# Strassen products chained in one PSUM bank with ScalarE copies, and another division of the preparing work

## The chip, the cores and the metric

The kernel runs on one core of a Trainium2 chip. Such a core has a matrix engine (TensorE, in the profile PE, its weight loads PEld), VectorE (DVE), ScalarE (ACT), GpSimd (POOL) and SyncE (SP), which work side by side, each through its own queue in order, and wait for one another through semaphores. Operands lie in SBUF (128 partitions); TensorE writes its products into the eight banks of PSUM. The metric is the device time of one execution in microseconds, lower is better.

## The reference

An attention layer feeds a layer of experts:

```
scores = q k^T / 8 in a window of +-15, joined with 24 block scores (q against the maximum of k over 32 rows)
a      = softmax(scores);  attn = a [v; mean of v over blocks]        # batch 4, 8 heads, 768 rows, 64 wide
x      = attn as (3072, 512)
noisy  = x w_gate + log1p(exp(x w_noise)) * noise                     # (3072, 8)
top2, weights = the two largest of noisy per row, softmax over the two
for e in range(8):
    for the rows whose top2 holds e:
        h = relu(x[rows] @ w1[e])                                     # 512 -> 1024
        out[rows] += weight * (h @ w2[e])                             # 1024 -> 512
```

All inputs and outputs are float32.

## The kernel before

**Attention and routing** fill the first part. They write x to DRAM (`xd`) as a pair of 16-bit floats, high part and remainder, and make a table that lists, for every expert, the rows that it takes, with their weights. Each expert has 816 slots (`CAP`), in seven chunks of 128 rows, the last of 48.

**The expert part** runs over e = 0 to 7. Every 32-bit operand is a pair of 16-bit floats, a high one and a low one (`...h`, `...l`), and every product is made of three passes: high by high, low by high, high by low. For one expert:

- `x_gather` (GpSimd's queue, an indirect DMA into one of four buffers `xg`) and `x_trans` (SP's queue, a transposing DMA) bring x into `xte`, transposed, for two experts alternately.
- `w_load` (SP's queue) brings the weights in eight pieces through four staging buffers `stg`: w1 in four, then w2 in four.
- The first matmul, h = relu(x w1), uses one level of Strassen's scheme (Winograd's form) for experts 1 to 7: seven products of half-size blocks in place of eight. It needs sums of blocks of w1 (`ws`, split into `sh` and `sl`), and sums of blocks of x (`tt`, split into `tx`).
- The second matmul, y = h w2, goes chunk by chunk: three passes of eight matmuls (`mm2_turn`, line 890; line 887 for the last chunk). `y_out` (VectorE, line 913) multiplies by the row's weight and adds `prev`, what `out` held for those rows, which `prev_gather` has fetched by an indirect DMA of GpSimd's queue; `y_scatter` writes the rows back in the same way. The bank `pt` has two buffers, so a chunk waits for `y` of the chunk before last.

**The first matmul in detail.** `mm1_quad(e, f, tick)` makes group f (0 to 3), which is rows f and f+4 of h. A `product` is six matmuls of 128 x 408 columns. It calls products 1, 6, 5, 7, 4, 2, 3. Products 1 and 2 go to bank `a`, 6 and 7 to `b`, 5 and 3 to `d`, 4 to `c`, where the second of a pair adds onto the first:

```
p1 = copy(a)  after 1 (ScalarE);   u2 = b + p1  after 6;   u3 = b + p1  after 7  (VectorE)
c2 = [c + u3 | d + u3]  after 4;   c1 = d + u2  after 3
```

Product 7 adds into `b`, so TensorE has to wait until `u2` has been read from it. `h_split` then makes the high part of h (ScalarE, `relu`, line 815) and the low one (VectorE, line 818).

**The order of the work** is written by hand. After each product and after each pass of the second matmul a `tick` is counted: ticks 0 to 27 lie in the first matmul (28 = `M2`), 28 to 48 in the second. `put(e, k, f, ...)` hangs a call on tick k of expert e, and the instruction goes into its engine's queue there. So the next expert n = e+1 is prepared while e runs:

- `w1_sums` (lines 653 to 656): four sums on GpSimd for each of two pairs of pieces of w1, ticks 18 and 34.
- `w1_pair` (lines 669 and 671): high parts on ScalarE, low parts on VectorE, of plain blocks (part 0) and of sums (part 1).
- `t_diff` (line 688): GpSimd subtracts blocks of x, of the high and of the low part; `t_join`, `t_two` (line 676) and `t_four` (699 and 676) add on VectorE; `t_hi` (709, ScalarE) and `t_lo` (676, VectorE) split into `tx`.
- `STEPS` has fourteen groups of these calls. For n from 2 on the first two (`t_diff` of 3, high and low) sit at ticks 20 and 21, the other twelve at ticks 28 to 39, one on each.
- w1 is loaded in the first matmul, w2 at ticks 34, 35, 39 and 40, and split by `w_split` (lines 629 and 646) at ticks 3, 10, 17 and 24 of its own expert.
- x of n is gathered at ticks 1, 3, ... 13 of e's first matmul.

Expert 0 has plain matmuls without Strassen's scheme. Its ticks 3 to 10 follow the second half of its first matmul, 11 to 22 the passes of its chunks 3 to 6; expert 1 is prepared there.

Of the kernel before, what the change touches and what calls it, by code (L numbers as in the profile page):

```python
# [20 lines left out]
P = 128  # L21
# [39 lines left out]
def attn_moe(ctx, tc, qt, kt, vt, wgn, noise, w1, w2, out):  # L61
# [586 lines left out]
    WS_ = {}  # L648
# [9 lines left out]
    def w1_pair(e, k, part):  # L658
        w = WT[e]
        hi, lo = w["w1h"], w["w1l"]  # L660
        if part == 0:
            todo_ = [(hi[:, k, :HF], lo[:, k, :HF], SG[e, k][:, :HF]),
                     (hi[:, k + 2], lo[:, k + 2], SG[e, k + 2])]
        else:
            s = WS_[e, k]
            todo_ = [(w["sh"][:, :, k], w["sl"][:, :, k], s[:, 0:3]),
                     (hi[:, k, HF:], lo[:, k, HF:], s[:, 3])]
        for h, _, x in todo_:
            nc.scalar.activation(h, x, AF.Copy, scale=W1S)  # L669
        for h, l, x in todo_:  # L670
            nc.vector.scalar_tensor_tensor(l, x, W1S, h, op0=OP.mult, op1=OP.subtract)  # L671
# [3 lines left out]
    def plus(o, a, b, op=OP.add):  # L675
        nc.vector.scalar_tensor_tensor(o, a, 1.0, b, op0=OP.mult, op1=op)  # L676

    def tt(e, j):
        TT[e, j] = side_pool[0].tile([P, 2, HC], F32, name="tt", bufs=3)
        return TT[e, j]  # L680
# [4 lines left out]
    def t_diff(e, j, low):  # L685
        i = (1, 1) if j == 3 else (0, 1)
        o = (0, 1) if j == 3 else (0, 0)
        nc.gpsimd.tensor_tensor(tt(e, (j, low)), xb(e, *i, low), xb(e, *o, low), op=OP.subtract)  # L688
# [16 lines left out]
    def t_of(e, j):  # L705
        return TT[e, (j, 0)] if j in (1, 3) else TT[e, 2]
# [106 lines left out]
    def h_split(f, c0, c1, c, hook=None):  # L813
        hh, hl = HT
        nc.scalar.activation(hh[:, f, c0:c1], c, AF.Relu)  # L815
        if hook:
            hook()
        nc.vector.scalar_tensor_tensor(hl[:, f, c0:c1], c, 0.0, hh[:, f, c0:c1], op0=OP.max, op1=OP.subtract)  # L818

    def mm1_quad(e, f, tick):  # L820
        def temp(name, n=HC):
            return side_pool[0].tile([P, n], F32, name=name)

        a = accs[0].tile([P, 512], F32, name="a")[:, :HC]
        product(a, e, f, 1, True, False)
        p1 = temp("p1")
        nc.scalar.activation(p1, a, AF.Copy)  # L827
        tick()
        b = bank()[:, 0, :HC]
        product(b, e, f, 6, True, False)  # L830
        u2 = temp("u2")
        nc.vector.tensor_add(u2, b, p1)  # L832
        tick()
        d = bank()[:, 0, :HC]
        product(d, e, f, 5, True, False)
        tick()
        product(b, e, f, 7, False, True)
        u3 = temp("u3")
        nc.vector.tensor_add(u3, b, p1)  # L839
        c2 = temp("c2", 2 * HC)  # L840
        nc.vector.tensor_add(c2[:, HC:], d, u3)
        tick()
        c = bank()[:, 0, :HC]
        product(c, e, f, 4, True, True)
        nc.vector.tensor_add(c2[:, :HC], c, u3)  # L845
        h_split(f + FC // 2, 0, CAP, c2)
        tick()
        product(a, e, f, 2, False, True)
        h_split(f, 0, HC, a)
        tick()  # L850
        product(d, e, f, 3, False, True)
# [53 lines left out]
    def y_out(e, c, pv):  # L905
        py = PY[c]
        d = HD if c == LAST else DM
        y = side_pool[0].tile([P, DM], F32, name="y", bufs=4)[:, :d]
        gw = (TL[:, e] if c == LAST else tb_of(e, c)).bitcast(F32)[:, 1:2]
        if pv is None:  # L910
            nc.vector.tensor_scalar(y, py[:, :d], gw, None, op0=OP.mult)
        else:
            nc.vector.scalar_tensor_tensor(y, py[:, :d], gw, pv[:, :d], op0=OP.mult, op1=OP.add)  # L913
        y_scatter(e, c, y)
# [293 lines left out]
    STEPS = (
        ((t_diff, 3, 0),),
        ((t_diff, 3, 1),),  # L1210
        ((t_alloc,), (t_join, 3), (t_hi, 3)),
        ((t_two, 0),),
        ((t_two, 1), (t_lo, 3), (t_hi, 2)),
        ((w1_pair, 0, 0), (t_diff, 1, 0)),
        ((t_lo, 2), (t_diff, 1, 1)),
        ((w1_pair, 0, 1),),
        ((t_four,), (t_hi, 4)),
        ((t_lo, 4),),
        ((w1_pair, 1, 0),),
        ((t_join, 1), (t_hi, 1)),  # L1220
        ((w1_pair, 1, 1),),
        ((t_lo, 1),),
    )

    def steps(e, where, ks):
        for k, fs in zip(ks, STEPS):
            for f, *a in fs:
                put(where, k, f, e, *a)
# [5 lines left out]
    put(0, 8, w1_sums, 1, 0)  # L1234
    steps(1, 0, (9, 9, 10, 10, 11, 12, 12, 13, 14, 15, 16, 17, 19, 20))
    put(0, 13, w1_sums, 1, 1)
    for i, k in enumerate((14, 15, 20, 21)):
        put(0, k, w_load, 1, 4 + i)
    M2 = 7 * (FC // 2)
    for e in range(1, E):  # L1240
        put(e, 0, w2_alloc, e)
        for i in range(4):
            put(e, 7 * i + 3, w_split, e, 4 + i)
        if e + 1 == E:
            break
        n = e + 1
        put(e, 0, w1_alloc, n, True)
        for i, c in enumerate((0, 2, 1, 3)):
            put(e, 7 * i + 5, w_load, n, c)
        for c in range(NCH):  # L1250
            put(e, 2 * c + 1, gather, n, c)
        put(e, 18, w1_sums, n, 0)
        put(e, M2 + 6, w1_sums, n, 1)
        steps(n, e, (20, 21, *range(M2, M2 + 12)))
        for i, k in enumerate((6, 7, 11, 12)):
            put(e, M2 + k, w_load, n, 4 + i)

# [17 lines left out]
    for e in range(1, E):  # L1275
# [7 lines left out]
        for f in range(FC // 2):  # L1283
            mm1_quad(e, f, ticks)
# [8 lines left out]
    def over_chunk(e, c):  # L1293
# [28 lines left out]
        y = side_pool[0].tile([P, DM], F32, name="y", bufs=4)  # L1322
# [3 lines left out]
    def over_table():  # L1326
# [71 lines left out]
```

## Time and profile before

| | us |
|---|---|
| median of 3 runs (lowest, highest) | 798.98 (795.14, 802.47) |
| the profiled execution | 801.18 |
| its span, first to last instruction | 799.4 |
| TensorE busy | 668.0 (84%) |
| VectorE busy | 523.0 (65%) |
| GpSimd busy | 406.8 (51%) |
| ScalarE busy | 287.2 (36%) |
| mean granted clock of TensorE | 0.954 of full |

The expert part with Strassen's scheme begins at 236.2 us and ends at 788.4. The profile is of one execution. In a list of waits a row reads: the engine with its tile and line that waited, what released it, then the total, the number of times and the longest, all in us. In the order of time a row is: start, duration, engine, line, operation, output and inputs, shape, number of merged instructions, and in brackets the idle time before it with what ended that. In a list of groups the number after the comma is the mean duration in ns. A duration runs to an instruction's last write, so successive instructions of one engine overlap a little.

### The profile page before, as it was taken

How to read it: one execution, taken by the hardware profiler on the slowest of the kernel's cores; microseconds unless marked ns; L12 is line 12 of the kernel's file. 1: busy time of each engine (PE TensorE's matmuls, PEld its weight loads, DVE VectorE, ACT ScalarE, POOL GpSimd, SP SyncE). 2: the span in 40 equal slices, each digit the busy share in tenths (PEclk: the TensorE clock that was granted, in tenths of full speed). 3: DMA queues.
4: the chain of work that ended last, by engine and by line, in shares of the span. 5: the costliest groups of instructions: out<-in, count | busy, mean ns of one | idle time of the engine just before them, and what ended most of it. 6: DMA issues, size and time to landing. Idle time of an engine off the chain costs nothing.

```text
span 799.4 us, 14010 instructions
## 1 busy us (share of the span) xinstructions
PE 668.0 (84%) x5400; PEld 373.8 (47%) x5400; DVE 523.0 (65%) x873; ACT 287.2 (36%) x594; POOL 406.8 (51%) x519
## 2 busy tenths in 40 slices
PE   7998888899558796989698879796979797979894
PEld 6776666555234442544254335442544353435442
DVE  6667988972286785578557855685568657855610
ACT  3888888412043332233223222332233223312300
POOL 3444355034674656547644764656465656652041
PEclk9999999999978999999899999998999899989998
DMA  8999997777537443754366437343634374431020
GB/s 281 304 292 307 301 285 225 233 244 163 149 110 189 101 143 119 158 131 137 111 150 131 131 122 168 106 144 119 164 92 156 120 177 107 145 105 53 0 93 31
DMA packets 100295, 125.89 MB, mean 157 GB/s; under 512 B 58985, under 2 KB 63857, under 8 KB 100220
## 3 DMA queue, kind: packets, MB, share of 16 engines
q1 hardware_dynamic: 88076, 88.64, 39.9%
q0 software_dynamic: 12144, 36.28, 15.1%
q8 instruction: 44, 0.72, 0.4%
q14 instruction: 31, 0.25, 0.1%
HBM read 87.57 MB, written 26.21 MB: 142 GB/s over the span
## 4 chain that ended last, share of the span: by engine, by line
DVE 31%; PE 29%; issue 14%; ACT 13%; DMA 6%; POOL 5%; SPq 0%; POOLq 0%; DVEq 0%; ACTq 0%
PE pt L890 12%; PE h L809 6%; DVE htl L818 5%; ACT hth L815 4%; DVE tt L676 4%; DVE w1l L671 3%; DVE w2l L646 3%; PE pt L887 2%; POOL tt L688 2%; PE h L773 2%; ACT p L310 2%; ACT tx L709 2%; DVE u L839 2%; DVE sl L671 2%; DMA xte<-xg 2%
## 5 line engine op out<-in xcount | busy, mean ns | idle before, releaser
L890 PEld LDWEIGHTS <-hth 128*128 128x128 f16 x768 | 78.7, 103 | 166.4 <-issue 85.7
L890 PE MATMUL pt<-w2h,hth 128*128 128x512 f16 x376 | 102.7, 420 | 59.9 <-DVE y L913 43.4
L92 POOL DMA_INDIRECT out_dram<-y,tb x48 | 66.6, 1388 | 138.0 <-DVE y L913 124.2
L809 PE MATMUL h<-tx,sh 128*128 128x408 f16 x336 | 82.3, 344 | 36.4 <-DVE u L832 34.1
L92 POOL DMA_INDIRECT xg<-xd,tb x56 | 61.1, 1091 | 87.8 <-DMA xte<-xg 46.9
L815 ACT ACTIVATE hth<-c 128x816 f16<-128x816 f32 (+1 forms) x56 | 39.9, 713 | 175.4 <-DVE c L845 85.9
L890 PE MATMUL pt<-w2l,hth 128*128 128x512 f16 x376 | 93.2, 393 | 0.0
L890 PE MATMUL pt<-w2h,htl 128*128 128x512 f16 x376 | 88.8, 379 | 0.0
L818 DVE SCALAR_TENSOR_TENSOR htl<-c,hth 128x816 f16<-128x816 f32 (+1 forms) x56 | 52.3, 934 | 43.7 <-ACT hth L815 43.7
L709 ACT ACTIVATE tx<-tt 128x816 f16<-128x816 f32 x28 | 24.7, 883 | 137.1 <-DVE tt L676 137.1
L913 DVE SCALAR_TENSOR_TENSOR y<-pt,tb,prev 128x512 f32<-128x512 f32 x42 | 31.3, 745 | 61.5 <-PE pt L890 58.5
L809 PEld LDWEIGHTS <-sh 128*128 128x128 f16 x336 | 33.4, 99 | 66.5 <-issue 41.2
L809 PEld LDWEIGHTS <-w1h 128*128 128x128 f16 x448 | 43.9, 99 | 35.3 <-issue 3.8
L890 PEld LDWEIGHTS <-htl 128*128 128x128 f16 x384 | 37.6, 98 | 45.3
L671 DVE SCALAR_TENSOR_TENSOR w1l<-stg,w1h 128x512 f16<-128x512 f32 (+1 forms) x28 | 55.2, 1994 | 5.4 <-ACT w1h L669 5.4
L358 POOL TENSOR_TENSOR xr<-x,xr 128x512 f16<-128x512 f32 x22 | 25.6, 1164 | 63.5 <-ACT xr L351 31.3
L809 PE MATMUL a<-xte,w1h 128*128 128x408 f16 x224 | 57.6, 339 | 0.0
L92 POOL DMA_INDIRECT prev<-out_dram,tb x42 | 49.4, 1176 | 10.4 <-issue 9.5
L688 POOL TENSOR_TENSOR tt<-xte 128x816 f32<-128x816 f16 x28 | 52.2, 1884 | 4.1 <-DVE tx L676 1.9
L310 ACT ACTIVATE p<-s,nm 128x118 f32<-128x118 f32 x192 | 53.4, 377 | 0.8
L809 PE MATMUL h<-tx,sl 128*128 128x408 f16 x168 | 44.2, 344 | 1.3 <-DVE sl L671 1.3
L827 ACT ACTIVATE p<-a 128x408 f32<-128x408 f32 x28 | 13.9, 496 | 82.5 <-issue 67.7
(202 smaller groups left out, 1269.7 us busy)
## 6 DMA issues: line engine op xcount, KB each, us to landing
stg<-in_w_dram SPq DMA_DIRECT2D x64, 512.0 KB
hth<-in_vt_dram SPq DMA_DIRECT2D x8, 780.0 KB
vw<-in_vt_dram SPq DMA_DIRECT2D x32, 195.0 KB
q<-in_qt_dram SPq DMA_DIRECT2D x24, 256.0 KB
xd<-xr SPq DMA_DIRECT2D x24, 256.0 KB
out_dram<-xg SPq DMA_DIRECT2D x8, 768.0 KB
kb<-in_kt_dram SPq DMA_DIRECT2D x6, 768.0 KB
htl<-in_vt_dram SPq DMA_DIRECT2D x16, 195.0 KB
```

The lines of the kernel that those rows point to most:

```text
L92: return nc.gpsimd.indirect_dma_start(**kw)
L310: nc.scalar.activation(PE_[t][:, a, hp, :], SC[t][:, a, hp, :], AF.Exp, bias=NM[t][:, 1, a, hp:hp + 1], scale=0.125)
L358: engine.tensor_tensor(XR[t][:, DM:], X[t], XR[t][:, 0:DM], op=OP.subtract)
L671: nc.vector.scalar_tensor_tensor(l, x, W1S, h, op0=OP.mult, op1=OP.subtract)
L676: nc.vector.scalar_tensor_tensor(o, a, 1.0, b, op0=OP.mult, op1=op)
L688: nc.gpsimd.tensor_tensor(tt(e, (j, low)), xb(e, *i, low), xb(e, *o, low), op=OP.subtract)
L709: nc.scalar.activation(TX[e][:, 0, j - 1], t_of(e, j), AF.Copy)
L809: nc.tensor.matmul(o, lhs[a][:, c], rhs[b][:, c], start=start and n == 0, stop=stop and n == 5, skip_group_check=True)
L815: nc.scalar.activation(hh[:, f, c0:c1], c, AF.Relu)
L818: nc.vector.scalar_tensor_tensor(hl[:, f, c0:c1], c, 0.0, hh[:, f, c0:c1], op0=OP.max, op1=OP.subtract)
L890: nc.tensor.matmul(py, hx[:, f, c * P:c * P + P], w[:, f, :], start=first, stop=final, skip_group_check=True)
L913: nc.vector.scalar_tensor_tensor(y, py[:, :d], gw, pv[:, :d], op0=OP.mult, op1=OP.add)
```

## The change

- **The products.** `mm1_quad` is replaced by `mm1_all`, which makes all four groups of an expert and interleaves them by the list `ROUNDS` (a negative number is a product of the group before). Products 1, 6, 7 and 4 add up in one bank X. After 1, 6 and 7 ScalarE copies the sum so far out (`P1`, `U2`, `U3`); after 4 the bank is a block of the result. Product 2 has its own bank A, to which VectorE adds `P1` in place; 5 and 3 share DD: after 7 VectorE writes `C22` = DD + `U3` to SBUF, after 3 it adds `U2` to DD in place. The high and low parts of h are made from these in pieces of 408 columns, `h_hi` on ScalarE and `h_lo` on VectorE, at places named in the list.
- **The sums of weights** move from GpSimd to VectorE (`plus`, four instructions for a pair, in two parts), and `w1_pair` is divided into `w1_hi` and `w1_lo`.
- **The order.** For n from 2 on `t_diff` and `t_join` lie wholly in the first matmul; the rest of the preparation lies at ticks 28 to 42. For expert 1, in expert 0, the same work lies at ticks 8 to 18.
- **x sooner.** For experts 3 to 7 x is gathered and transposed one stage earlier, in the second matmul of the expert two before. Expert 2's stays in expert 1's first matmul, at ticks 0, 2, ... 12.
- **Buffers.** The `tt` buffers have a name each, so the two low differences share one; `y` has three buffers in place of four. The loads of w2 move to ticks 37, 38, 42 and 43.

```diff
-    def w1_sums(e, k):
+    def w1_sums(e, k, part):
         a, b = SG[e, k], SG[e, k + 2]
-        s = WS_[e, k] = side_pool[0].tile([P, 4, HF], F32, name="ws")
-        nc.gpsimd.tensor_tensor(s[:, 0], a[:, HF:], b[:, HF:], op=OP.add)
-        nc.gpsimd.tensor_tensor(s[:, 2], a[:, :HF], a[:, HF:], op=OP.subtract)
-        nc.gpsimd.tensor_tensor(s[:, 1], s[:, 0], a[:, :HF], op=OP.subtract)
-        nc.gpsimd.tensor_tensor(s[:, 3], b[:, :HF], s[:, 1], op=OP.subtract)
+        if part == 0:
+            s = WSUM[e, k] = side_pool[0].tile([P, 4, HF], F32, name="ws")
+            plus(s[:, 0], a[:, HF:], b[:, HF:])
+            plus(s[:, 2], a[:, :HF], a[:, HF:], OP.subtract)
+        else:
+            s = WSUM[e, k]
+            plus(s[:, 1], s[:, 0], a[:, :HF], OP.subtract)
+            plus(s[:, 3], b[:, :HF], s[:, 1], OP.subtract)
...
+    def h_hi(f, c0, c1, c):
+        nc.scalar.activation(HT[0][:, f, c0:c1], c, AF.Relu)
+
+    def h_lo(f, c0, c1, c):
+        nc.vector.scalar_tensor_tensor(HT[1][:, f, c0:c1], c, 0.0, HT[0][:, f, c0:c1], op0=OP.max, op1=OP.subtract)
+
+    ROUNDS = ((1, 2, 6, 5, 7), (1, 2, -4, 6, 5, -3, 7), (1, 2, -4, 6, 5, -3, 7), (1, -4, 6, 5, 7, -3, 4, 2, 3))
+
+    def mm1_all(e, tick):
...
+        def after(f, p):
+            g = f + FC // 2
+            if p == 1:
+                P1[f] = temp("p1")
+                nc.scalar.activation(P1[f], X[f], AF.Copy)
+                if f:
+                    h_hi(g - 1, HC, CAP, C22[f - 1])
+            elif p == 2:
+                nc.vector.tensor_add(A[f], A[f], P1[f])
+                if f:
+                    h_lo(g - 1, HC, CAP, C22[f - 1]) if f < 3 else None
+                h_hi(f, 0, HC, A[f])
+            elif p == 4:
+                h_hi(g, 0, HC, X[f])
+            elif p == 6:
+                U2[f] = temp("u2", 2)
+                nc.scalar.activation(U2[f], X[f], AF.Copy)
+            elif p == 3:
+                nc.vector.tensor_add(DD[f], DD[f], U2[f])
+                h_hi(f, HC, CAP, DD[f])
+            elif p == 7:
+                U3[f] = temp("u3")
+                nc.scalar.activation(U3[f], X[f], AF.Copy)
+                C22[f] = temp("c22")
+                nc.vector.tensor_add(C22[f], DD[f], U3[f])
...
+                o = DD[f] if p in (3, 5) else A[f] if p == 2 else X[f]
+                product(o, e, f, p, p in (1, 5, 2), p in (4, 3, 2))
+                after(f, p)
...
-        y = side_pool[0].tile([P, DM], F32, name="y", bufs=4)[:, :d]
+        y = side_pool[0].tile([P, DM], F32, name="y", bufs=3)[:, :d]
...
+    steps(1, 0, (
+        (8, w1_sums, 0, 0), (8, w1_hi, 0, 0), (8, w1_sums, 0, 1), (9, t_diff, 3, 0), (9, t_diff, 3, 1),
+        (9, w1_hi, 0, 1), (9, w1_lo, 0, 0), (10, w1_lo, 0, 1), (11, w1_sums, 1, 0), (11, t_alloc),
+        (11, t_join, 3), (11, t_diff, 1, 0), (11, t_diff, 1, 1), (11, t_hi, 3), (12, w1_sums, 1, 1),
+        (12, w1_hi, 1, 0), (12, t_two, 0), (13, t_two, 1), (13, t_hi, 2), (13, w1_lo, 1, 0),
+        (14, t_lo, 3), (14, t_join, 1), (14, w1_hi, 1, 1), (15, t_lo, 2), (15, t_hi, 1), (16, t_four),
+        (16, t_hi, 4), (17, t_lo, 1), (18, t_lo, 4), (18, w1_lo, 1, 1)))
...
-        for c in range(NCH):
-            put(e, 2 * c + 1, gather, n, c)
...
+        if e == 1:
+            for c in range(NCH):
+                put(e, 2 * c, gather, n, c)
+        d = (16, 18, 20, 22) if e == 1 else (4, 7, 12, 15)
+        steps(n, e, (
+            (d[0], t_diff, 3, 0), (d[1], t_diff, 3, 1), (d[1] + 3, t_join, 3),
+            (d[2], t_diff, 1, 0), (d[3], t_diff, 1, 1), (d[3] + 4, t_join, 1)))
+        steps(n, e, [(M2 + k, *a) for k, *a in (
+            (0, t_alloc), (0, t_two, 0), (0, t_hi, 3), (1, t_two, 1), (1, t_hi, 1), (2, t_lo, 3), (2, t_hi, 2),
+            (3, w1_sums, 0, 0), (3, w1_hi, 0, 0), (4, w1_sums, 0, 1), (5, t_lo, 2), (5, w1_hi, 0, 1),
+            (6, w1_lo, 0, 0), (7, t_four), (8, w1_lo, 0, 1, (0,)), (8, t_hi, 4), (9, w1_lo, 0, 1, (1,)),
+            (9, t_lo, 1), (10, w1_sums, 1, 0), (10, w1_hi, 1, 0), (11, w1_sums, 1, 1), (11, t_lo, 4),
+            (12, w1_lo, 1, 0), (12, w1_hi, 1, 1), (13, w1_lo, 1, 1, (0,)), (14, w1_lo, 1, 1, (1,)))])
...
+        if e + 2 < E:
+            for c in range(NCH):
+                put(e, M2 + 3 * c + 1, gather, e + 2, c)
...
-        for f in range(FC // 2):
-            mm1_quad(e, f, ticks)
+        mm1_all(e, ticks)
```

More of the change, by code (lines that the diff above doesn't have):

```diff
@@ L661, in w1_pair, with w1_hi, w1_lo @@
         if part == 0:
[L662 to L668, printed above, removed]
+            return ((hi[:, k, :HF], lo[:, k, :HF], SG[e, k][:, :HF]), (hi[:, k + 2], lo[:, k + 2], SG[e, k + 2]))
+        s = WSUM[e, k]
+        return ((w["sh"][:, :, k], w["sl"][:, :, k], s[:, 0:3]), (hi[:, k, HF:], lo[:, k, HF:], s[:, 3]))
+    def w1_hi(e, k, part):
+        for h, _, x in w1_parts(e, k, part):
             nc.scalar.activation(h, x, AF.Copy, scale=W1S)
-        for h, l, x in todo_:
+    def w1_lo(e, k, part, only=(0, 1)):
+        for i in only:
+            h, l, x = w1_parts(e, k, part)[i]
             nc.vector.scalar_tensor_tensor(l, x, W1S, h, op0=OP.mult, op1=OP.subtract)
     TX, TT = {}, {}
-    def plus(o, a, b, op=OP.add):
-        nc.vector.scalar_tensor_tensor(o, a, 1.0, b, op0=OP.mult, op1=op)
     def tt(e, j):
-        TT[e, j] = side_pool[0].tile([P, 2, HC], F32, name="tt", bufs=3)
+        TT[e, j] = side_pool[0].tile([P, 2, HC], F32, name=f"t{j}")
         return TT[e, j]
@@ L687, in t_diff @@
         o = (0, 1) if j == 3 else (0, 0)
-        nc.gpsimd.tensor_tensor(tt(e, (j, low)), xb(e, *i, low), xb(e, *o, low), op=OP.subtract)
+        nc.gpsimd.tensor_tensor(tt(e, 0 if low else j), xb(e, *i, low), xb(e, *o, low), op=OP.subtract)
     def t_join(e, j):
-        a = TT[e, (j, 0)]
-        plus(a, a, TT[e, (j, 1)])
+        plus(TT[e, j], TT[e, j], TT[e, 0])
     def t_two(e, low):
-        plus(TT[e, 2] if low else tt(e, 2), TT[e, 2 if low else (3, 0)], xb(e, 0, 0, low))
+        plus(TT[e, 2] if low else tt(e, 2), TT[e, 2 if low else 3], xb(e, 0, 0, low))
     def t_four(e):
@@ L1206, in gather, with steps @@
         x_trans(e, c)
[L1208 to L1228, printed above, removed]
+    def steps(e, where, at_):
+        for k, f, *a in at_:
+            put(where, k, f, e, *a)
     for i, c in enumerate((0, 2, 1, 3)):
@@ L1233, in attn_moe @@
         put(0, 2 + c, gather, 1, c)
[L1234 to L1237, printed above, removed]
+    steps(1, 0, (
[5 more added lines that the diff above has]
+        (16, t_hi, 4), (17, t_lo, 1), (18, t_lo, 4), (18, w1_lo, 1, 1)))
+    for i, k in enumerate((14, 15, 19, 20)):
         put(0, k, w_load, 1, 4 + i)
@@ L1249, in attn_moe @@
             put(e, 7 * i + 5, w_load, n, c)
-        for c in range(NCH):
-            put(e, 2 * c + 1, gather, n, c)
[L1252 to L1255, printed above, removed]
+        if e == 1:
[11 more added lines that the diff above has]
+            (12, w1_lo, 1, 0), (12, w1_hi, 1, 1), (13, w1_lo, 1, 1, (0,)), (14, w1_lo, 1, 1, (1,)))])
+        for i, k in enumerate((9, 10, 14, 15)):
             put(e, M2 + k, w_load, n, 4 + i)
+        if e + 2 < E:
+            for c in range(NCH):
+                put(e, M2 + 3 * c + 1, gather, e + 2, c)
     for c in range(3):
```

92 lines of the change are left out of this document (45 added, 47 removed).

## The prediction

> **What bounds the kernel now.** I read the page's first line, then TensorE's waits, then busy time by stage, and last the order of time inside one stage.
>
> ```profile
> span 799.4 us, 14010 instructions
> ```
> ```profile
> PE pt L890 <- DVE y L913: 43.4, 15, 5.2
> PE h L809 <- DVE u L832: 34.1, 21, 3.0
> PE pt L890 <- DVE y L911: 14.1, 1, 14.1
> ```
>
> The profiled execution took 801.18 us for this span, 1.8 us more; it is 2.2 us above the median of the runs (798.98). Nearly all that TensorE waits for is VectorE: in the second matmul for `y` (it empties a bank that the next chunk but one needs), in the first for `u2` (the add that reads bank `b` before product 7 accumulates into it). Both are in the expert part, so I cut that into stages. First the seven first-matmul stages (28 products each, experts 1 to 7), then the six second-matmul stages that have another expert's preparation beside them. Columns: stretch, length, busy time of PE, PEld, DVE, ACT and POOL, granted clock, DMA share, GB/s.
>
> ```profile
> 236.20:279.40 43.20, 34.31 (x170) 17.72 (x169) 28.88 (x40) 14.90 (x22) 23.50 (x29) 0.88 0.56 149
> 322.10:356.10 34.00, 29.40 (x170) 16.40 (x169) 22.08 (x32) 10.96 (x17) 15.28 (x20) 1.00 0.74 153
> ...
> sum 250.10, PE 212.40 PEld 116.49 DVE 162.58 ACT 81.48 POOL 116.89; mean PE 30.34 PEld 16.64 DVE 23.23 ACT 11.64 POOL 16.70
> ```
> ```profile
> 279.40:322.10 42.70, 35.99 (x195) 16.98 (x193) 29.69 (x28) 10.79 (x13) 25.87 (x30) 0.96 0.39 127
> ...
> sum 268.10, PE 222.26 PEld 102.81 DVE 185.92 ACT 70.40 POOL 172.53; mean PE 37.04 PEld 17.14 DVE 30.99 ACT 11.73 POOL 28.75
> ```
>
> 250.1 and 268.1 us, without a break from 236.2 to 754.4. What would they take if TensorE never waited? In order of time, expert 3's first matmul:
>
> ```profile
> 407.94 0.51 PE L809 MATMUL a<-xte,w1h 128*128 128x408 f16 x2
> ...
> 410.01 0.51 PE L809 MATMUL a<-xte,w1h 128*128 128x408 f16 x2
> ...
> 414.61 0.51 PE L809 MATMUL h<-tx,sh 128*128 128x408 f16 x2 [1.33 <-DVE u L832]
> ```
>
> Two products lie between the first two rows: 1.035 us each, 28 of them 29.0 us. The third row is the recurring gap of a group of seven. For the second matmul the last expert, which has nothing to prepare, gives the floor (the chain's last two rows): 31.09 + 2.76 = 33.85 us.
>
> ```profile
> 754.55 31.09 PE pt L890 x144
> 785.63 2.76 PE pt L887 x48
> ```
>
> So the first stages hold 250.1 - 203.0 = 47.1 us above their floor, the second 268.1 - 203.1 = 65.0 us: 112 us is the most that both can give. Why is VectorE late in the second? Expert 3's second matmul, all engines in order of time:
>
> ```profile
> 449.55 3.42 POOL L688 TENSOR_TENSOR tt<-xte 128x816 f32<-128x816 f16 x2
> ...
> 449.70 4.35 DVE L671 SCALAR_TENSOR_TENSOR w1l<-stg,w1h 128x1024 f16<-128x1024 f32 x1 [0.25 <-ACT w1h L669]
> ...
> 454.90 0.74 DVE L913 SCALAR_TENSOR_TENSOR y<-pt,tb,prev 128x512 f32<-128x512 f32 x1
> 455.56 1.74 DVE L671 SCALAR_TENSOR_TENSOR sl<-ws,sh 128x1536 f16<-128x1536 f32 x1
> 455.69 1.84 PE L890 MATMUL pt<-w2h,hth 128*128 128x512 f16 x4 [3.09 <-DVE y L913]
> 455.92 2.27 POOL L92 DMA_INDIRECT out_dram<-y,tb  x1 [2.93 <-DVE y L913]
> ```
>
> A 1024-wide split took 4.35 us beside two GpSimd subtractions; the same form has a mean of 1.318 us on line 646 (below). It ended about when they did plus its own length. `y` stands in VectorE's queue behind it, and TensorE behind `y`. Beside a descriptor-writing GpSimd instruction (455.92) VectorE's split took its usual 1.74 us, and it is GpSimd that grew, to 2.27.
>
> **A stall costs twice.** After a long wait the eight matmuls of a pass run slow:
>
> ```profile
> 225.61 3.57 PE L890 MATMUL pt<-w2h,hth 128*128 128x512 f16 x8 [14.06 <-DVE y L911]
> ...
> 231.45 1.89 PE L890 MATMUL pt<-w2h,htl 128*128 128x512 f16 x8
> ```
>
> 3.57 against 1.89 us, which is why the granted clock is 0.88 in the stage above that starts badly. A removed wait of 3 us or more is worth up to 1.7 us more than itself; the stage sums contain this already.
>
> **The change, part by part.** *The first matmul.* Before, bank `b` takes 6 and then 7, and 7 waits for an add of VectorE that waits in turn for ScalarE's copy. After, bank X takes 1, 6, 7, 4; after each of the first three ScalarE copies it out, and another product lies between each product and the next one into X: 2 (and 4 of the group before) between 1 and 6, 5 (and 3) between 6 and 7, two or more between 7 and 4. Does a copy fit behind one product? The chain and ScalarE's queue at expert 3's start:
>
> ```profile
> 402.82 1.14 PE a L809 x6
> ```
> ```profile
> 404.06 0.51 ACT L827 ACTIVATE p<-a 128x408 f32<-128x408 f32 x1 [14.79 <-PE a L809]
> ```
>
> The copy ends at 404.57, 1.75 us after the product began; two products take 2.07. It fits with 0.3 us over in the first group; the later ones mostly have 1.03 more. ScalarE's load per group is 7 x 0.51 plus one 1.05 us split, about 4.6 of 7.25 us. VectorE does three adds and four 408-wide lows in place of five adds, one 816-wide low and two 408-wide ones: 7 x 0.58 = 4.1 us a group.
>
> ```profile
> L646 DVE SCALAR_TENSOR_TENSOR w2l<-stg,w2h 128x1024 f16<-128x1024 f32 x32 | 41.9, 1318 | 0.0
> ...
> L839 DVE TENSOR_TENSOR u<-h,p 128x408 f32<-128x408 f32 x28 | 16.3, 582 | 39.4 <-PE h L809 39.4
> ...
> L671 DVE SCALAR_TENSOR_TENSOR w1l<-ws,w1h 128x512 f16<-128x512 f32 x14 | 9.5, 681 | 0.0
> L699 DVE SCALAR_TENSOR_TENSOR tt<-tt,xte 128x816 f32<-128x816 f32 x7 | 7.0, 994 | 0.0
> ```
>
> Two of the three adds now write PSUM in place, which no row shows; between 0.49 us (a shorter write path) and 0.994 (a row twice as wide), I take the 0.58 of the row nearest in shape; at the upper end VectorE has 3.3 us more in a stage of 29, still beside TensorE. A stage's VectorE work is then 4 x 4.1 + 4 x 1.32 + two 0.99 joins = 23.7 us of 29. What is late next is ScalarE behind VectorE: the high half of A waits for the add, and the copy of 6 stands behind it. The four subtractions of `t_diff` now all lie here, 3.42 us for two, and a `w2l` split that meets them can wait as the row at 449.70 did, up to 3.4 us; from the end of product 2 to the start of 7 lie two products in the first group and four later (4.1 us), less 1.1 us for the high half and the copy. I take 1.0 us of loss per stage (0 to 3): 30.0. Expert 1 gets its successor's x only during this stage, since its gathers stay there, so its joins come late: 3 us, 32.0. First stages: 32 + 6 x 30 = 212.0, a gain of 38.1.
>
> *The second matmul.* Eight weight sums come to VectorE from GpSimd. No row has an f32 sum there; the nearest is 512 wide with two SBUF operands, 0.681 us; bounds 0.58 and 0.994. 8 x 0.681 = 5.4 us per expert (4.6 to 8.0). The two joins leave (-2.0). So VectorE gets, per expert: weight lows 2 x (0.681 + 1.318 + 1.74 + 0.681) = 8.8; four x lows, `t_two` twice and `t_four`'s two, 8 x 0.994 = 8.0; sums 5.4; seven `y` at most 0.74 each, 5.2: 27.4 us, as against a measured 30.99 with the clashes. Before, the preparation sits in the first 12 passes; after, in the first 15. Those are 15 x 31.09/18 = 25.9 us of TensorE. In them VectorE has 27.4 less two `y`, plus four short leftovers of the first matmul, 2.3: 28.2 us by durations. Its instructions overlap a little (454.90 + 0.74 is 455.64, the next began at 455.56): 0.08 x 30 = 2.4 us less, 25.8. That is even with TensorE, and two banks give one chunk, 5.2 us, of slack. GpSimd does no arithmetic in this stage any more, only descriptors, beside which VectorE kept its speed. I take 1.0 us per stage (0 to 6): 34.8. Second stages: 6 x 34.8 = 208.8, a gain of 59.3.
>
> By the Trainium skill (Perfetto Trace Analysis, Optimizing Scalar/DVE Operations) offloading between GpSimd and VectorE "might not help", as they share a read port. That speaks against moving the sums, and by it the second stages would stay at 268.1. The skill's SBUF — State Buffer (Who interferes with whom) is finer: a VectorE instruction with two SBUF inputs contends with a GpSimd one that reads SBUF, not with one that only writes; with it the rows at 449.70 and 455.56 both agree.
>
> *x sooner.* Seven gathers (GpSimd queue, with a memset each) and seven transposes (SP queue) of expert e+2 move from e+1's first matmul to e's second. On GpSimd they stand between the scatters and `prev` gathers, so they wait when `y` is late, and the `w2` loads on SP stand behind three of the transposes.
>
> ```profile
> L92 POOL DMA_INDIRECT out_dram<-y,tb x48 | 66.6, 1388 | 138.0 <-DVE y L913 124.2 <-DVE y L911 6.6 <-DVE sl L671 4.4
> ```
>
> 7 gathers, 7 scatters, 4 `prev`: 18 x (1.39 + about 0.3 between) = 30 us of 34, off TensorE's path while `prev` is three chunks ahead; at the 2.27 of the row above it would be 46 us, and the last `prev` late. I cost it at nothing, hidden by those three buffers; what it buys is that `t_diff` can start in the first matmul. The third `y` buffer less makes `y` wait for a scatter three chunks (15 us) old: nothing.
>
> *Expert 0.* Its preparation is also spread, but the subtractions wait for x as now:
>
> ```profile
> 211.64 3.40 POOL L688 TENSOR_TENSOR tt<-xte 128x816 f32<-128x816 f16 x2 [0.94 <-DMA xte<-xg]
> ```
>
> The join at pass 11 stands ahead of `y` of chunk 3, so that `y` cannot come before 215. Four 1 us steps and a clash of 3.4 follow it before `y` leaves: some 222, where TensorE restarted at 225.6. Gain 3.2 (bounds 0 and 9, when the sums no longer delay GpSimd): the first matmul of expert 1 at 233.0.
>
> **Sum:** 233.0 + 212.0 + 208.8 + 45.0 (754.4 to the end, unchanged) = 698.8, with the 1.8 outside 700.6: 100.6 below the profiled 801.18. From the median 798.98 that is **698 us**. With every stage at its floor it is 684, with 2 us more loss in all 13 stages 724.
>
> **Rivals.** *VectorE too late in the second matmul.* Its balance is exact to a few us and rests on no clash; waits for ScalarE's high halves in between would break it. For: the measured 30.99 us busy hardly changes, only the length it is spread on. Against: the chunk in hand. If half the loss stays, (44.7 - 33.85)/2 = 5.4 in place of 1.0, six times 4.4: 725. *ScalarE takes VectorE's place in the first matmul*: the copies queue behind high halves that wait for VectorE, 3 us more in seven stages as the row at 414.61 had per expert: 719; with the one before 746. Against: the margins above. *Moving the sums gives nothing* (the clashes' saving and the sums cancel): only 38.1 + 3.2 gained, 758; the row at 449.70 is against it. This is what the skill's sentence on offloading would have one expect. *Slower:* the gathers put descriptor writing all along the second matmul, and if that locks VectorE out as arithmetic does, its 22.2 us of SBUF work grow by 4.35/1.318 = 3.3 to 73, with `y` 78 a stage, 6 x 34 over now, less 41: some 960. It decides once a stage exceeds 44.7 + 41.3/6 = 51.6 us. The row at 455.56 is against it.
>
> **Chances:** forecast 0.58 (own range 684 to 712), VectorE late 0.20, ScalarE 0.08, both 0.05, sums neutral 0.05, slower 0.04. Range 680 to 748. About 1% (8 us) is what this kernel's runs can tell from no change: faster 0.93, within 0.03, slower 0.04.
>
> **What would show it.** Right: TensorE's waits for `u` gone, those for `y` under 10 us in all; 28 products in 30 us; second matmuls near 34 with VectorE near 30 busy; splits of 1024 at 1.3 us there. Wrong: waits of TensorE for ScalarE's copies, `y` still late after the eighth pass, `prev` landing after its chunk, or the clock at half in the first matmul.

## The result, and the profile after

The changed kernel takes 710.4 us in the median of four runs (708.8 to 718.7); the kernel before, beside it, 798.6. The ratio is 0.891, with a 95% interval of 0.884 to 0.898. The forecast was 698, the range 680 to 748.

The first profile of the changed kernel is of its slowest run (718.7 us, span 716.9). A second one, of the same kernel run again (709.6 us median, ratio 0.888, 0.882 to 0.894), has a span of 708.0 us, close to the median, so the stages are read from it; the first is called in where the two differ. TensorE's waits in the second profile (what released it, total us, times, longest):

```profile
PE pt L928 <- DVE y L949: 7.8, 1, 7.8
PE h L813 <- DVE c L855: 7.1, 1, 7.1
PE pt L928 <- ACT hth L818: 4.3, 7, 0.6
PE pt L366 <- ACT pts L319: 3.6, 9, 0.9
PE h L813 <- DVE htl L821: 3.5, 5, 2.7
PE h L813 <- ACT u L853: 3.5, 7, 0.5
```

The 43.4 us for `y` in experts 1 to 7 are gone from the list, and so are the 34.1 us for `u2`. What is left are two long waits at the beginning (line 949 is `y` of expert 0; line 855 is the `C22` add in expert 1), one of 2.7 us in expert 5 (line 821), and small ones for ScalarE, 0.5 to 0.6 us per expert. The stages, first matmuls and then second ones; the columns are those of the prediction's tables of stages:

```profile
232.60:270.50 37.90, 30.28 (x170) 16.70 (x169) 19.64 (x30) 15.07 (x29) 16.97 (x23) 0.93 0.60 133
305.90:335.90 30.00, 29.35 (x171) 16.44 (x170) 18.00 (x28) 15.42 (x29) 14.00 (x16) 1.00 0.50 143
...
499.90:532.50 32.60, 29.41 (x172) 16.49 (x170) 20.59 (x28) 15.42 (x29) 14.61 (x16) 1.00 0.49 133
...
sum 220.20, PE 206.08 PEld 115.37 DVE 129.95 ACT 107.59 POOL 90.56; mean PE 29.44 PEld 16.48 DVE 18.56 ACT 15.37 POOL 12.94
```
```profile
270.50:305.90 35.40, 34.80 (x193) 16.67 (x191) 30.27 (x39) 12.06 (x16) 25.17 (x39) 0.98 0.76 214
335.90:370.60 34.70, 34.08 (x193) 16.46 (x192) 28.70 (x38) 11.70 (x15) 21.35 (x31) 1.00 0.72 188
...
sum 208.90, PE 205.20 PEld 98.87 DVE 173.75 ACT 70.56 POOL 124.57; mean PE 34.20 PEld 16.48 DVE 28.96 ACT 11.76 POOL 20.76
```

Seven first matmuls: 220.2 us where they were 250.1. Six second matmuls: 208.9 where they were 268.1. In the second ones VectorE is busy nearly as long as before (28.96 us a stage against 30.99), but in 34.8 us instead of 44.7. The 1024-wide splits of w1, of which the prediction met one at 4.35 us, are short again (the group, with its mean in ns behind the comma):

```profile
L679 DVE SCALAR_TENSOR_TENSOR w1l<-stg,w1h 128x1024 f16<-128x1024 f32 x14 | 17.0, 1214 | 0.0
```

Before, the same group had a mean of 3017 ns.

### The profile page after: what moved, and what is told of

Same layout as the page of the kernel before. It is cut to its first block, busy times and chain, and to the rows that moved or that the text cites. A ratio compares the mean times of both kernels' runs of the same rounds, so it can differ in the third digit from the quotient of the medians.

```text
span 716.9 us, 14064 instructions
## 1 busy us (share of the span) xinstructions
PE 651.1 (91%) x5400; PEld 371.6 (52%) x5400; DVE 484.1 (68%) x901; ACT 316.5 (44%) x678; POOL 321.8 (45%) x463
## 4 chain that ended last, share of the span: by engine, by line
PE 56%; DVE 13%; ACT 9%; DMA 9%; issue 5%; POOL 4%; SPq 1%; POOLq 0%; DVEq 0%; ACTq 0%
PE pt L928 27%; PE h L813 16%; DMA xte<-xg 4%; PE a L813 2%; ACT p L310 2%; PE pt L925 2%; DMA xg<-xd,tb 2%; PE s L296 2%; ACT w2h L629 2%; POOL t L693 2%; PE o L329 2%; DVE t L649 1%; ACT hth L818 1%; DMA out_dram<-xg 1%; PE pt L316 1%
## 5 line engine op out<-in xcount | busy, mean ns | idle before, releaser
L928 PEld LDWEIGHTS <-hth 128*128 128x128 f16 x768 | 75.4, 99 | 109.4 <-issue 13.6
L928 PE MATMUL pt<-w2h,hth 128*128 128x512 f16 x376 | 93.6, 389 | 14.0 <-DVE y L949 6.7
L92 POOL DMA_INDIRECT xg<-xd,tb x56 | 65.4, 1168 | 59.9 <-DVE w2l L646 28.1
L693 POOL TENSOR_TENSOR t<-xte 128x816 f32<-128x816 f16 x28 | 49.9, 1799 | 56.5 <-DMA xte<-xg 31.5
L646 DVE SCALAR_TENSOR_TENSOR w2l<-stg,w2h 128x1024 f16<-128x1024 f32 x32 | 39.7, 1250 | 37.4 <-ACT w2h L629 29.7
L813 PE MATMUL h<-xte,w1h 128*128 128x408 f16 x224 | 57.7, 340 | 6.2 <-DVE c L855 6.2
L713 ACT ACTIVATE tx<-t 128x816 f16<-128x816 f32 x28 | 24.0, 880 | 57.6 <-DVE t L649 57.6
L818 ACT ACTIVATE hth<-h 128x408 f16<-128x408 f32 x56 | 28.3, 506 | 41.4 <-DVE h L849 41.2
L835 ACT ACTIVATE p<-h 128x408 f32<-128x408 f32 x28 | 14.3, 512 | 72.3 <-PE h L813 61.4
L674 ACT ACTIVATE sh<-ws 128x1536 f16<-128x1536 f32 x14 | 20.8, 1482 | 32.6 <-DVE ws L649 28.6
```

Source lines behind the costliest of these rows:

```text
L92: return nc.gpsimd.indirect_dma_start(**kw)
L646: nc.vector.scalar_tensor_tensor(lo, SG[e, i], sc, hi, op0=OP.mult, op1=OP.subtract)
L693: nc.gpsimd.tensor_tensor(tt(e, 0 if low else j), xb(e, *i, low), xb(e, *o, low), op=OP.subtract)
L713: nc.scalar.activation(TX[e][:, 0, j - 1], t_of(e, j), AF.Copy)
L813: nc.tensor.matmul(o, lhs[a][:, c], rhs[b][:, c], start=start and n == 0, stop=stop and n == 5, skip_group_check=True)
L818: nc.scalar.activation(HT[0][:, f, c0:c1], c, AF.Relu)
```

## The experiments

### The changed kernel once more

Edit: none.

> The changed kernel once more, unaltered, for a second profile. Theory (the first profile's 12 us over the forecast come half from code that the change does not touch, up to the second half of expert 0's first matmul, which began 6.7 us later than in the profile of before): the first matmul of expert 1 starts near 233 instead of 239.9, the span is near 707, and the stages of experts 2 and on measure 30.0 and 34.7 us again. Rival (the change itself delays the start): 240 again, span near 717.

Measured: 709.6 us, span 708.0; expert 1's first matmul began at 232.6 us, and the stages of experts 2 on are within 0.4 us of the 30.0 and 34.7 us of the tables above, in both profiles, but for single first matmuls (30.8 and 33.3 us in the first profile, 32.6 in the second). What follows: of the 8.9 us between the two profiles 5.6 lie ahead of the code that was changed, 1.6 between there and expert 1's first matmul, and the rest in those single stages. The first matmul of expert 0 for its second half of rows began, in the order of time of the first and of the second profile, at

```profile
190.18 0.89 PE L777 MATMUL h<-xte,w1h 128*128 128x432 f16 x4 [0.84 <-ACT xte L764]
```
```profile
184.55 0.89 PE L777 MATMUL h<-xte,w1h 128*128 128x432 f16 x4 [0.58 <-ACT xte L764]
```

and over all the kernels of this study that place varied from 182.6 to 190.2 us, without an edit before it. So a single span of this kernel is good to some 8 us, and stages are the better measure.

### The sums of weights back on GpSimd

```diff
-            plus(s[:, 0], a[:, HF:], b[:, HF:])
-            plus(s[:, 2], a[:, :HF], a[:, HF:], OP.subtract)
+            nc.gpsimd.tensor_tensor(s[:, 0], a[:, HF:], b[:, HF:], op=OP.add)
+            nc.gpsimd.tensor_tensor(s[:, 2], a[:, :HF], a[:, HF:], op=OP.subtract)
...
```

> The changed kernel with its eight weight sums per expert back on GpSimd, at the same ticks. Theory (GpSimd arithmetic locks VectorE out, and GpSimd with 30 us of descriptors has no room for 8 x 1.3 to 2.1 us): the 1024-wide splits of the second matmul rise from 1.3 us to 2 and more, each second matmul from 34.7 to 38 to 45, the time to 730 to 770. Rival (moving the sums is neutral, clashes and sums cancel): within 8 us of the changed kernel.

Measured: 762.9 us (ratio 0.959, 0.953 to 0.966), 761.4 without the slowest of its four runs, which is some 51 us above the changed kernel. Its profile is of its fastest run (754.2 us). The second matmuls, and the groups of splits:

```profile
sum 247.10, PE 214.52 PEld 108.22 DVE 180.61 ACT 71.28 POOL 186.51; mean PE 35.75 PEld 18.04 DVE 30.10 ACT 11.88 POOL 31.09
```
```profile
L679 DVE SCALAR_TENSOR_TENSOR w1l<-stg,w1h 128x1024 f16<-128x1024 f32 x14 | 33.9, 2424 | 0.0
L679 DVE SCALAR_TENSOR_TENSOR sl<-ws,sh 128x1536 f16<-128x1536 f32 x14 | 25.4, 1814 | 25.8 <-ACT sh L674 25.8
```

Place for place in the order of time, two splits met two sums:

```profile
446.83 4.59 DVE L679 SCALAR_TENSOR_TENSOR w1l<-stg,w1h 128x512 f16<-128x512 f32 x2
447.83 1.28 POOL L657 TENSOR_TENSOR ws<-stg 128x512 f32<-128x512 f32 x1
449.06 1.27 POOL L658 TENSOR_TENSOR ws<-stg 128x512 f32<-128x512 f32 x1
```

What follows: moving the sums is worth 38 us in the second matmuls alone (247.1 against 208.9). VectorE was rid of 8 x 0.68 = 5.4 us per stage and was yet busy 1.1 us longer (30.10 against 28.96): the clashes cost it 6.6 us per stage. The same trace has both cases: of its fourteen 1024-wide splits the seven that met a sum or a subtraction of GpSimd took 2.74 to 3.99 us, the seven that met only its descriptor writing 1.21 to 1.22. The second part of the price is a wait: the splits of sums stood 25.8 us in all for ScalarE's high parts, which come after GpSimd's sums. GpSimd itself was not full, 31.1 us of 41.2. That the sums could have stayed on GpSimd at other ticks was not tried.

### The products in the old order

```diff
...
-        mm1_all(e, ticks)
+        for f in range(FC // 2):
+            mm1_quad(e, f, ticks)
```

with `mm1_quad` put back for `mm1_all`.

> The changed kernel with the seven products in the old order and banks (1, 6, 5, 7, 4, 2, 3, one group after the other, adds on VectorE; the last add is made in place in its bank, for lack of SBUF); order of preparation, sums and gathers as changed. Theory (product 7 waits for VectorE's add, some 1.3 us in three of four groups, more where a subtraction of GpSimd meets it): first matmuls 34 to 36 us instead of 30, the time 28 to 42 us above the changed kernel. Rival (the gain of the first matmul comes from the order of preparation and not from the chain): within 10 us of it.

Measured: 741.8 us (ratio 0.931, 0.926 to 0.937), 32 us above the changed kernel. Its longest wait, and then its first and its second matmuls:

```profile
PE h L813 <- DVE u L836: 40.6, 22, 7.0
```
```profile
sum 258.30, PE 217.47 PEld 118.12 DVE 168.37 ACT 77.92 POOL 94.41; mean PE 31.07 PEld 16.87 DVE 24.05 ACT 11.13 POOL 13.49
```
```profile
sum 203.40, PE 203.40 PEld 98.71 DVE 163.84 ACT 70.74 POOL 120.79; mean PE 33.90 PEld 16.45 DVE 27.31 ACT 11.79 POOL 20.13
```

The chain is worth 38 us in the first matmuls (258.3 against 220.2) and takes 5.5 us back in the second ones: with the old products these run at their floor, 33.9 us, with the new ones at 34.7, mostly because the last high halves of h come 0.6 us late (the wait for ScalarE at line 818).

### The chained products alone, in the kernel before

```diff
...
-        for f in range(FC // 2):
-            mm1_quad(e, f, ticks)
+        mm1_all(e, ticks)
```

with `mm1_all` put in for `mm1_quad`.

> The kernel before with the chained, interleaved products alone; order of preparation, sums on GpSimd, gathers as before. Theory (the two halves of the change act in different stages): TensorE's waits for u in the first matmul go (34.1 us in the profile of before), first matmuls 31 to 33 us apart from expert 1's, second matmuls stay at 43 to 47 us; the time falls by 15 to 30 us, to 767 to 782. Rival (the chain frees nothing, its gain needs the new order): within 8 us of before. By the forecast's term for the first matmul it would be 38 us, 759.

Measured: 782.3 us (ratio 0.978, 0.972 to 0.984), 16 us below the kernel before. First and second matmuls, and the longest wait:

```profile
sum 212.00, PE 205.96 PEld 115.40 DVE 117.30 ACT 110.59 POOL 82.95; mean PE 29.42 PEld 16.49 DVE 16.76 ACT 15.80 POOL 11.85
```
```profile
sum 288.70, PE 227.11 PEld 103.44 DVE 196.56 ACT 70.22 POOL 204.54; mean PE 37.85 PEld 17.24 DVE 32.76 ACT 11.70 POOL 34.09
```
```profile
PE pt L924 <- DVE y L947: 53.4, 16, 5.2
```

The first matmuls gave the sum of the prediction's term, a gain of 38.1 us, but not its parts: 34.2 us for expert 1 (32.0 in the forecast) and 29.6 for each of the others (30.0). The second ones grew from 268.1 to 288.7 us; the expectation had them unchanged, and missed that. VectorE's preparation is not what moved: its splits of w1 (line 671) are busy 12.9 us in a mean second matmul of both kernels, its sums and splits of x (line 676) 10.5. It is GpSimd's. Part of its subtractions and sums (lines 688 and 653 to 656) had run while TensorE stood in the first matmul; now that this stage is shorter, they rise from 12.0 to 16.3 us in a mean second matmul. `y` then waits 11.8 us in all for `prev`, which GpSimd's queue fetches (3.0 before), and VectorE's work on x 9.0 us for GpSimd. TensorE's waits for `y` grow by 10 us (53.4 against 43.4) and those for ScalarE's high halves by 6 (8.7 against 2.3), and it is busy 5 us longer (227.1 against 222.3) at a granted clock of 0.89 to 0.93 in place of 0.92 to 0.96. Together that is about the 20.6 us. The chain alone is worth 16 us and the rest alone (the run above) 54, each against the kernel before beside it; together they give 87 to 88.

### Every gather in the first matmul before

```diff
-        if e == 1:
-            for c in range(NCH):
-                put(e, 2 * c, gather, n, c)
-        d = (16, 18, 20, 22) if e == 1 else (4, 7, 12, 15)
+        for c in range(NCH):
+            put(e, 2 * c, gather, n, c)
+        d = (16, 18, 20, 22)
```

with the gathers in the second matmul left out.

> The changed kernel with every expert's x gathered in the first matmul of the expert before, at ticks 0 to 12, and the differences at ticks 16 to 22 with their joins behind, as the changed kernel has it for expert 2 alone. Theory (x then lands too late for the joins, and VectorE, which stands at a join, holds up the add that product 3 waits for): the five first matmuls of experts 2 to 6 grow from 30 to 34 to 38, 20 to 40 us in all. The prediction's reckoning (the place of the gathers costs nothing by itself): no more than 8 us above.

Measured: 730.6 us (ratio 0.915, 0.909 to 0.920), 21 us above the changed kernel. The first matmuls grew by 11 us in all (231.2), those of experts 2 to 6 to 31.6 to 33.7 us, less than expected (34 to 38); the second ones grew by 10 (218.9). The wait that grew is the one at line 855, where VectorE makes `C22`:

```profile
PE h L813 <- DVE c L855: 20.1, 6, 6.1
```

So the sooner gathers, with the sooner differences and joins that they allow, are worth 21 us, against the 8 us at most that the prediction's reckoning left; the run does not part the two.

### Every sum made twice

```diff
             plus(s[:, 0], a[:, HF:], b[:, HF:])
+            plus(s[:, 0], a[:, HF:], b[:, HF:])
...
```

> The changed kernel with every weight sum made twice on VectorE (the second writes the same again): 8 x 0.68 = 5.4 us more VectorE work in each of six second matmuls and in expert 0. Theory (VectorE keeps pace and has most of a chunk, 5.2 us, in hand; the fifth y came 1.1 us late in the second profile without a wait of TensorE): second matmuls 34.7 to 36.5 us, the time up by 3 to 15 us. Rival (VectorE is the bound of the second matmul): every us is paid, 40 us a stage, 32 us and more above the changed kernel.

Measured: 728.5 us (ratio 0.913, 0.908 to 0.917), 19 us above. A second matmul of it:

```profile
343.60:379.80 36.20, 34.09 (x193) 16.51 (x191) 33.99 (x46) 11.86 (x15) 19.39 (x27) 1.00 0.64 164
```

5.3 us more of VectorE cost 1.5 us, as expected of a stage that has most of a chunk in hand: VectorE is not the bound there, but stands 4 us from being it (TensorE now waits for `y`, 9.5 us in all). The total was missed all the same (3 to 15 us expected): the five stages make 7.9; the rest lies in expert 1's second matmul (39.2 us against 35.4), in a start 4.5 us later than in the second profile, part of which can be the variation above, and in the first matmuls, 4.5 us longer in all.

### The copies on VectorE

```diff
-                nc.scalar.activation(P1[f], X[f], AF.Copy)
+                nc.vector.tensor_copy(P1[f], X[f])
...
```

the same for `U2` and `U3`.

> The changed kernel with the three copies of each group on VectorE instead of ScalarE: 12 x 0.58 = 7.0 us more VectorE work in each first matmul, 23.7 + 7.0 = 30.7 of 29. Theory (the chain is free because ScalarE has room and VectorE has not): first matmuls 33 to 36 us in place of 30, the time 20 to 42 us up. Rival (the gain is the interleaving, and the engine that copies does not matter): within 8 us.

Measured: 739.4 us (ratio 0.928, 0.920 to 0.937), 30 us above, all of it in the first matmuls (249.8 us against 220.2):

```profile
PE h L813 <- DVE u L853: 28.3, 15, 3.6
```

Experts 1 to 4 took 36.7 to 37.7 us, a little more than expected. The interleaving alone does not free TensorE; the copies have to be on the engine that has room.

### Expert 2's x in expert 0's stage

```diff
+    for c in range(NCH):
+        put(0, 13 + c, gather, 2, c)
...
-        if e == 1:
-            for c in range(NCH):
-                put(e, 2 * c, gather, n, c)
-        d = (16, 18, 20, 22) if e == 1 else (4, 7, 12, 15)
+        d = (4, 7, 12, 15)
```

> The changed kernel with x of expert 2 gathered in expert 0's stage (ticks 13 to 19) in place of expert 1's first matmul, and its differences at ticks 4 to 15 like the other experts'. Theory (expert 1's first matmul takes 37.9 us because its successor's x lands late, the joins hold VectorE, and product 3 waits for VectorE's add, 7.1 us): it falls to 30 to 32 us, the time to 700 to 704, unless the extra gathers delay expert 1's own x. Rival (it is long because of expert 1's own preparation, which is late at its start): it stays above 36 us, the time within 3 us of the changed kernel.

Measured: 710.5 us (ratio 0.890, 0.885 to 0.895); expert 1's first matmul still took 39.1 us. Its order of time:

```profile
255.08 5.08 POOL L693 TENSOR_TENSOR t<-xte 128x816 f32<-128x816 f16 x3 [4.86 <-DMA xte<-xg]
258.52 2.52 DVE L649 SCALAR_TENSOR_TENSOR t<-t,t 128x816 f32<-128x816 f32 x1 [4.93 <-POOL t L693]
262.07 0.84 PE L813 MATMUL h<-tx,sh 128*128 128x408 f16 x2 [6.68 <-DVE htl L821]
```

GpSimd waited for x until 255.1, VectorE at the join for GpSimd until 258.5, TensorE until 262.1. The subtractions that wait for x began 17.7 us after the stage did (29.4 in the changed kernel's second profile), but this edit had also moved the joins to ticks 10 and 19, so the wait stayed. By its measure the rival was right; the profile pointed to the join, hence the next run.

### The same with the joins later

```diff
-        d = (4, 7, 12, 15)
+        if e == 1:
+            steps(n, e, ((22, t_diff, 3, 0), (22, t_diff, 3, 1), (23, t_diff, 1, 0), (25, t_join, 3),
+                         (25, t_diff, 1, 1), (28, t_join, 1)))
...
```

> As the run with x of expert 2 gathered in expert 0's stage, and in expert 1's stage the joins of expert 2's differences moved from ticks 10 and 19 to 25 and 28. In that run the joins at tick 10 waited for x that landed at 255, 17.5 us after the first matmul began. Theory (expert 1's long first matmul is a join placed ahead of x's landing, with the adds of the products behind it on VectorE): the wait of 6.7 us goes, the first matmul of expert 1 falls to 30 to 32 us, the time to 700 to 705. Rival (its length is expert 1's own late preparation and the clock): above 35 us still, 709 to 712.

Measured: 707.5 us (ratio 0.886, 0.883 to 0.888). Expert 1's first matmul:

```profile
238.60:268.80 30.20, 29.33 (x170) 16.44 (x169) 18.68 (x29) 15.43 (x29) 11.01 (x12) 1.00 0.77 198
```

The 8 us are gone, and the cause of that stage is settled: a join ahead of x's landing. The time fell by 2 to 3 us only, where 5 to 10 had been expected. In the profile that stage began at 238.6 in place of 232.6, and 5.5 of these 6 us lie at the place of the earlier variation, which stood at 190.1. Against the changed kernel's first profile, where that place stood at 190.2 too, the span is 12.6 us shorter (704.3 against 716.9). Why the median of the runs shows so little of this stays open.

### Expert 0's order

```diff
-        (11, t_join, 3), (11, t_diff, 1, 0), (11, t_diff, 1, 1), (11, t_hi, 3), (12, w1_sums, 1, 1),
...
+        (11, t_diff, 1, 0), (11, w1_hi, 1, 0), (12, w1_sums, 1, 1), (12, w1_hi, 1, 1),
+        (13, w1_lo, 1, 0), (14, w1_lo, 1, 1),
+        (16, t_join, 3), (16, t_diff, 1, 1), (16, t_hi, 3), (16, t_two, 0),
...
```

> The changed kernel with expert 1's preparation in another order in expert 0: the weight sums and splits first (ticks 8 to 14), the joins of x not before tick 16, behind y of chunks 3 and 4, which stood behind a join that waited for x to land. Theory (VectorE stands at the join and y behind it, 7 us of wait and a slow clock after it): the wait for y at line 949 goes, the first matmul of expert 1 starts 6 to 11 us earlier, near 222 to 227, but waits up to 4 us for its sums of x; the time 2 to 8 us lower, part of it lost again at the joins of expert 2. Rival (x lands too late for anything but waiting): the start moves by under 2 us.

Measured: 709.0 us (ratio 0.888, 0.885 to 0.890). The wait of 7 us for `y` became 1.7, expert 1's first matmul began at 223.8, and then took 44.1 us: product 6 waited 6.1 us for ScalarE's copy of product 1, `C22` cost 5.5 more, and the granted clock was 0.86 in the stage. So 6.2 of the 8.8 us gained at the start were lost again in this stage, and the time did not fall by the 2 to 8 us expected; the subtractions of expert 1's x began at 211.7, when x landed, and the high parts that stand ahead of that copy wait for them.

### All three, and the gathers of experts 3 to 7 closer together

```diff
-                put(e, M2 + 3 * c + 1, gather, e + 2, c)
+                put(e, M2 + 2 * c, gather, e + 2, c)
```

besides the three edits above.

> Both together, and x of experts 3 to 7 gathered at every second tick instead of every third of the second matmul, to land before the next first matmul's joins. Theory: first matmuls of 30.0 us throughout (the profiles of the changed kernel show one of 32.5 to 33.3 among experts 2 to 6), start of expert 1 near 225; 235 + 6 x 30 + 6 x 34.7 with the rest as it is gives 690 to 698. Rival (gathers nearer together hold up the scatters and the loads of w2 on their queues): second matmuls longer than 35 us, the time no lower than 705.

Measured: 705.7 us (ratio 0.882, 0.879 to 0.884), where 690 to 698 had been expected. The first matmuls of experts 3 to 6 are all 30.0 us, and the second matmuls from expert 2 on 34.7. That does not show that the closer gathers removed the single longer ones: in the two runs with expert 2's x sooner, which have the old spacing, they were at most 30.3 as well. Expert 1's first matmul took 40.8: ScalarE's copy stood behind a high part that waited for GpSimd's last subtraction, and that behind gathers (the start of the subtraction, and TensorE):

```profile
225.71 1.73 POOL L693 TENSOR_TENSOR t<-xte 128x816 f32<-128x816 f16 x1
```
```profile
233.38 0.84 PE L813 MATMUL h<-tx,sh 128*128 128x408 f16 x2 [7.87 <-ACT p L835]
```

### The same with expert 2's gathers later in GpSimd's queue

```diff
-        put(0, 13 + c, gather, 2, c)
+        put(0, (17, 17, 18, 18, 19, 20, 21)[c], gather, 2, c)
```

> The three edits together, with the gathers of expert 2's x in expert 0's stage moved from ticks 13 to 19 to ticks 17 to 21. In the profile of the three together product 6 of expert 1 waited 7.9 us for ScalarE's copy of product 1, which stood behind a high part of x's sums; those waited for the last subtraction of GpSimd (started at 225.7, behind gathers in its queue). Theory (GpSimd's queue order is what holds expert 1's sums): the subtraction starts by 222, product 6 waits 2 to 4 us, expert 1's first matmul ends 4 to 6 us earlier, the time falls to 699 to 703. Rival (expert 1's own x lands too late for any order to help, the waits only move): within 2 us of 705.6.

Measured: 702.3 us (699.9 to 703.1; ratio 0.878, 0.875 to 0.881), the fastest of all, by the ratios 1.1 to 1.5% below the two measurements of the changed kernel. The subtraction began at 223.2, and product 6 still waited 6.0 us; the stage took 37.9 us. Of the 2.5 us by which the subtraction moved, 1.9 are seen in that wait. The time is within the expected 699 to 703, but the wait is not the 2 to 4 us that were to bring it there, and how much of expert 1's start is left to x's own landing stays open.

## Why the prediction was right, and by how much it was off

The prediction's sum has four terms inside the span; beside them the second profile (span 708.0 where the sum said 698.8):

| term | forecast | measured |
|---|---|---|
| expert 1's first matmul begins | 233.0 | 232.6 |
| seven first matmuls | 212.0 | 220.2 |
| six second matmuls | 208.8 | 208.9 |
| from there to the end | 45.0 | 46.3 |

- **Expert 1's start** came out as forecast in this profile: TensorE took up work again at 221.7 us, "some 222" in the prediction, after a wait of 7.8 us for `y` in place of 14.1. In the first profile the stage began at 239.8, so that 233.0 and 232.6 lie so close is in part luck.
- **The second matmul** came out as the steps had it: 34.7 us a stage against 34.8, VectorE 28.96 us busy against a count of 27.4 and 2.3 of leftovers, the sums at 0.68 to 0.80 us each against 0.681, the 1024-wide split at 1.21. But the loss of 0.85 us, for which 1.0 stood in the sum, is not that of late `y`: 0.6 of it is the wait for ScalarE's last high halves, which the sum did not have. That size is right by luck. That removing the clash mattered is shown by the run with the sums on GpSimd.
- **The first matmul** of experts 2 to 7 was right as well, 30.0 us and 29.7 for the last. The adds in place took 0.585 us, where 0.58 was taken; the shorter write path of the lower bound, 0.49, was not seen. But the 1.0 us of loss in a stage stood there for the clash of `w2l` with the subtractions, and in the plain stages there was none: the four splits of the stage at 305.9 were busy 4.42 us together. TensorE waited 0.5 us for `U3` on ScalarE and 0.15 behind a join on VectorE instead, so this size too is luck.
- **The step that was mis-sized** is expert 1: "its joins come late: 3 us". It was 8.9 (37.9 us in all, 38.1 in the first profile). The mechanism was named, but not followed to its end: VectorE did not only come late, it stood 8.5 us at the join, and product 3, which adds into the bank that `C22` is read from, stood behind it:

```profile
262.03 5.07 POOL L693 TENSOR_TENSOR t<-xte 128x816 f32<-128x816 f16 x3 [11.51 <-DMA xte<-xg]
265.46 2.52 DVE L649 SCALAR_TENSOR_TENSOR t<-t,t 128x816 f32<-128x816 f32 x1 [8.48 <-POOL t L693]
...
268.52 0.84 PE L813 MATMUL h<-xte,w1h 128*128 128x408 f16 x2 [7.12 <-DVE c L855]
```

- **"x sooner" costed at nothing** was not quite so: in each profile one first matmul (32.6 and 33.3 us) waited for x, since its last gather goes out at the end of the second matmul. The chain of the first profile shows such a landing, 12.5 us from the start of the gather's transfer to the first subtraction:

```profile
572.80 5.63 DMA xg<-xd,tb
578.45 6.70 DMA xte<-xg
585.31 4.40 POOL t L693 x2
```

With the gathers at every second tick no first matmul of experts 3 to 6 was longer than 30.0 us, but two runs without that edit had none above 30.3 either. The run with every gather back in the first matmul puts the whole of this part at 21 us.
- **The step from the profiled run to the median** took 2.2 us off, as it had been before; the second profile of the changed kernel lies at its median. These 2 us, 8.2 for the first matmuls and 1.3 at the end make up nearly all of the 12 by which 698 missed 710.
- **The rivals.** VectorE too late in the second matmul: no, though only 4 us away from it (the doubled sums). ScalarE in VectorE's place: 0.5 us per expert, not 3. Sums neutral: refuted by the run with the sums on GpSimd. Slower, by descriptor writing that locks VectorE out: no, the 1024-wide splits took 1.21 us beside it. By the Trainium skill (Perfetto Trace Analysis, Optimizing Scalar/DVE Operations) moving work between these two engines might not help; here it was worth some 51 us. The Trainium skill's page SBUF — State Buffer (Who interferes with whom) has a VectorE instruction with two SBUF inputs contend with a GpSimd one that reads SBUF, and the splits in the run with the sums on GpSimd agree: 2.74 us and more beside its arithmetic, 1.21 without.

## What to carry to other kernels

Take the copies that free an accumulating bank to the engine with room, and put another product between each product and the next into the same bank; but look at once where the time saved goes, since work that another engine did beside the shortened stage now falls into the next one (the chain alone kept 16 of its 38 us). An instruction that waits for data in an in-order queue costs everything behind it, so a step belongs behind the landing of its data and not only ahead of its use. Elementwise work on two operands from SBUF was cheaper here all on VectorE than shared with GpSimd at the same time; whether that holds when the two are kept apart was not tried.

## What the runs showed of the hardware that was not expected

GpSimd's descriptor writing, which left VectorE's instructions at their length, can itself be stretched beside them: in the kernel before one `DMA_INDIRECT` took 2.27 us beside a 1.74 us split, while the 28 scatters of `y` in that profile that met next to no VectorE instruction took 0.98 to 1.02. So the prediction's row at 455.56 speaks for VectorE's side alone. A clash can outlast one GpSimd instruction: the 1024-wide split that took 4.35 us began beside two subtractions that followed one another, 3.42 us together, and ended 1.08 us after both; two splits in the run with the sums on GpSimd ended 1.1 us after two sums. And code that no edit touched began its next stage between 182.6 and 190.2 us from one profile to the next, more than the effect of several of the edits.
